# A later weight load, a fused x+1 and traced plan durations in an attention + MoE kernel

## The chip, the cores and the metric

The kernel runs on one core of one Trainium2 chip. The time is the device time of one execution in microseconds (us); most of what follows concerns differences of 1 to 13 us in about 1000. A profile is one execution with every instruction recorded; TensorE is PE there, its weight loads are PEld, VectorE is DVE, ScalarE is ACT, GpSimd is POOL, and SP is the engine that issues most DMAs.

## The reference, cut

```python
def phi(x): return np.where(x > 0, x, np.exp(x) - 1.0) + 1.0
q_p, k_p = phi(q), phi(k)                      # 8 batches, 8 heads, 576 tokens, 64 wide
kv = einsum('bhsd,bhde->...'); z = k_p.sum(2)  # linear attention
attn = num / (den + 1e-6)
x = attn as (4608, 512)
P = exp(x @ w_gate - max); 8 x: P /= P.sum(1); P /= P.sum(0); P *= N / E   # Sinkhorn
for e in range(8):                             # MoE, every expert on every token
    out += P[:, e:e+1] * (relu(x @ w1[e]) @ w2[e])
```

phi(x) is max(x + 1, min(exp(x), 1)), which is how the kernel computes it.

## The kernel before

A small planner in the kernel (`_Plan.run`) takes tasks with an engine, a planned duration, dependencies and a priority, plays them through in planned time and emits the instructions of each engine in that order. In the traces each engine works through its own stream in that order and waits for real data (a step shown below has TensorE stand 0.58 us at a column sum, with ready matmuls behind it). So a planned duration never delays anything by itself; it decides **where an instruction stands in its engine's stream**. If the plan believes that something is ready too early, the real engine stands still at that place, with ready work behind it.

The 16 attention steps `att(b, g)` (8 batches, two halves of the heads) have priority; expert 0's two layers fill TensorE in between; the Sinkhorn chain follows; then experts 1 to 7 run to the end. The parts that the change touches:

```python
for nm, ten in (("k", k), ("q", q), ("v", v)):        # the loads of step n; n = 2, 3 (batch 1) on POOL
    ti = fadd(("pool", 1.0) if n in (2, 3) else ("sp", 0.45), fn, acq=[gr], prio=pr,
              deps=[w_last[0] if n in (2, 3) else None, in_prev[0]])
# ... phi: exponential on ACT; x+1 on ACT or DVE; then min and max on DVE
def f_t(e, ...):                                       # x + 1
    if e == "dve": nc.vector.tensor_scalar(out=o, in0=gin[nm]["tile"], scalar1=1.0, ..., op0=ALU.add)
    else:          nc.scalar.add(out=o, in_=gin[nm]["tile"], add=1.0)
def f_m(_, ...):
    nc.vector.tensor_scalar(out=ge["tile"], in0=ge["tile"], scalar1=1.0, ..., op0=ALU.min)
    nc.vector.tensor_tensor(out=o, in0=o, in1=ge["tile"], op=ALU.max)
tt_ = fadd({"dve": 0.75, "act": 1.17}, f_t, ...)
tph[nm] = fadd(("dve", 1.15), f_m, deps=[te, tt_], ...)
# ... Sinkhorn, 8 times: f_a on DVE, f_c the column-sum matmul on TensorE, f_d on DVE
a = add(("dve", 2.1), f_a, ...); c = add(("pe", 0.2), f_c, ..., lat=0.2); last = [add(("dve", 0.5), f_d, ...)]
# ... the weights of expert 0: both matrices right behind batch 0
w_t = {0: load_w1(0, prio=-290.0, parts=2, deps=[vcast[0]]) + load_w2(0, prio=-280.0, parts=2, deps=[vcast[1]])}
```

The softmax here doesn't subtract the row's maximum and nothing guards it: scores larger than these inputs give would overflow.

## Time and profile before

| | before |
|---|---|
| time, median of 4 runs | 1007.62 us |
| span of the profiled run | 1005.3 us |
| TensorE busy | 970.7 us (97%) |
| TensorE idle, 23.2 to 140 us (29.30 + 87.50 less 23.51 + 83.94) | 9.35 us |
| first matmul of expert 1 starts at | 205.6 us |

TensorE is the bound. A caution about "busy": matmuls are pipelined. Four 512-column matmuls of one group take 0.863 us of TensorE's time when others follow, but the timeline shows such a group as some 1.03 us long, its end being modelled.

### The profile page before, as it was taken

The page shows a single profiled execution, that of the slowest core. Times are in us where ns is not written, and L with a number is a line of the kernel's source. Part 1 is how long each engine was busy: PE and PEld are TensorE (multiplying, and loading weights), DVE is VectorE, ACT ScalarE, POOL GpSimd, SP SyncE. Part 2 cuts the span into 40 slices and gives each one's busy share as a digit, 9 for nine tenths or more (in the row PEclk, how much of TensorE's full clock was granted, in tenths as well). Part 3 has the DMA queues.
Part 4 walks back from the last instruction along what each step waited for, and adds up shares of the span by engine and source line. Part 5 has one row for each costly group of instructions (what it writes and reads, how often), then busy time and mean ns, then how long its engine had stood idle before and what let it go on. Part 6 is the DMA issues. An engine that isn't in the chain of part 4 may idle for free.

```text
span 1005.3 us, 21388 instructions
## 1 busy us (share of the span) xinstructions
PE 970.7 (97%) x8716; PEld 791.7 (79%) x8716; DVE 773.5 (77%) x1555; ACT 566.9 (56%) x1040; POOL 132.5 (13%) x171
## 2 busy tenths in 40 slices
PE   7799998999999999999999999999999999999997
PEld 3456564478888888888888888888888888888885
DVE  6889869768777977788777977788777977777774
ACT  4888853565555555564555555555555555555552
POOL 4211100011111111111111111111111111111110
PEclk9999999999999999999999999999999999999999
DMA  9977953162223622272223522272223522226663
GB/s 262 331 260 248 265 150 127 62 121 75 74 74 89 143 74 75 74 158 74 74 75 95 138 74 74 75 158 74 75 75 101 131 75 74 75 89 163 160 162 100
DMA packets 47027, 121.98 MB, mean 121 GB/s; under 512 B 4176, under 2 KB 18000, under 8 KB 46928
## 3 DMA queue, kind: packets, MB, share of 16 engines
q1 hardware_dynamic: 32128, 99.76, 30.1%
q0 software_dynamic: 14480, 20.33, 11.4%
q8 instruction: 68, 1.11, 0.4%
q10 hardware_dynamic: 320, 0.52, 0.1%
q14 instruction: 31, 0.25, 0.1%
HBM read 119.69 MB, written 17.69 MB: 137 GB/s over the span
## 4 chain that ended last, share of the span: by engine, by line
PE 83%; DVE 13%; ACT 2%; issue 1%; DMA 0%; DVEq 0%; ACTq 0%
PE ye L797 31%; PE hq L618 22%; PE att L618 10%; PE Zye L618 5%; PE Zye L797 5%; PE ye L694 4%; PE hq L527 3%; ACT Zye L630 1%; DVE xn L369 1%; DVE xst L559 1%; DVE S L770 1%; DVE tq L275 1%; DVE tk L275 1%; DVE h L647 1%; PE xt_ps L380 1%
## 5 line engine op out<-in xcount | busy, mean ns | idle before, releaser
L811 DVE SCALAR_TENSOR_TENSOR acc<-ye,P_sb,acc 128x256 f32<-128x256 f32 x620 | 266.8, 478 | 90.7 <-PE ye L797 76.1
L618 PEld LDWEIGHTS <-W 128*128 128x128 f16 x2016 | 197.0, 98 | 34.3 <-issue 11.2
L797 PEld LDWEIGHTS <-S 128*128 128x128 f16 x1984 | 192.3, 98 | 27.4 <-DVE S L770 4.0
L797 PE MATMUL ye<-T,S 128*128 128x256 f16 x1488 | 192.6, 273 | 0.0
L821 POOL TENSOR_TENSOR acc<-acc,st 128x256 f32<-128x256 f32 x124 | 90.9, 753 | 639.2 <-ACT st L818 628.8
L618 PEld LDWEIGHTS <-w 128*128 128x128 f16 x1512 | 147.7, 98 | 21.4 <-issue 1.6
L797 PEld LDWEIGHTS <-h 128*128 128x128 f16 x1488 | 145.5, 98 | 17.2 <-issue 0.3
L618 PE MATMUL hq<-xs,W 128*128 128x256 f16 x1008 | 151.2, 273 | 6.5 <-ACT Zye L630 6.4
L618 PE MATMUL att<-xs,W 128*128 128x256 f16 x1008 | 151.2, 273 | 0.0
L618 PE MATMUL hq<-xs,w 128*128 128x256 f16 x1008 | 144.9, 272 | 1.0 <-DVE h L647 0.9
L644 ACT ACTIVATE h<-hq 128x512 f16<-128x512 f32 x126 | 76.3, 606 | 79.6 <-PE hq L618 79.6
L647 DVE CUSTOM_DVE_ANT_0 h<-att,s 128x512 f16<-128x512 f32 x126 | 86.6, 687 | 43.4 <-PE att L618 36.7
L770 DVE TENSOR_TENSOR S<-h 128x1024 f16<-128x1024 f16 x124 | 85.1, 686 | 40.9 <-ACT h L644 40.8
L641 ACT ACTIVATE h<-Zye 128x512 f16<-128x512 f32 x126 | 75.8, 602 | 53.8 <-PE Zye L618 53.8
L630 ACT COPY Zye<-hq 128x512 f32<-128x512 f32 x126 | 72.7, 577 | 57.7 <-PE hq L618 57.4
L638 ACT COPY s<-att 128x512 f32<-128x512 f32 x126 | 74.4, 590 | 46.3 <-PE att L618 46.1
L818 ACT ACTIVATE st<-Zye,P_sb 128x256 f32<-128x256 f32 x124 | 52.0, 470 | 75.1 <-PE Zye L797 75.1
L634 ACT COPY s<-hq 128x512 f32<-128x512 f32 x126 | 74.7, 593 | 25.1 <-PE hq L618 25.1
L647 DVE CUSTOM_DVE_ANT_0 h<-hq,s 128x512 f16<-128x512 f32 x126 | 86.2, 684 | 0.9 <-PE hq L618 0.3
L694 PE MATMUL ye<-w,h 128*128 128x512 f16 x320 | 76.8, 379 | 0.7 <-DVE acc L219 0.7
L618 PE MATMUL Zye<-xs,w 128*128 128x256 f16 x504 | 75.6, 273 | 0.0
L527 PE MATMUL hq<-xT,w 128*128 128x512 f16 x288 | 70.6, 379 | 0.3 <-ACT h L531 0.3
(90 smaller groups left out, 972.4 us busy)
## 6 DMA issues: line engine op xcount, KB each, us to landing
xs<-xd SPq DMA_DIRECT2D x63, 896.0 KB, 4.6
w<-in_moe_w_dram POOLq DMA_DIRECT2D x14, 1024.0 KB, 10.8
out_dram<-acc SPq DMA_DIRECT2D x68, 128.0 KB, 2.4
kin<-in_k_dram SPq DMA_DIRECT2D x14, 576.0 KB, 5.5
qin<-in_q_dram SPq DMA_DIRECT2D x14, 576.0 KB, 5.0
vin<-in_v_dram SPq DMA_DIRECT2D x14, 576.0 KB, 6.2
xd<-xst SPq DMA_DIRECT2D x9, 512.0 KB, 2.6
xd<-xT SPq DMA_DIRECT2D x9, 256.0 KB, 5.1
```

The costliest lines, as they stand in the source:

```text
L527: nc.tensor.matmul(ghq["tile"], lhsT=gw1["tile"][:, c, ts(f, P)], rhs=xT[:, c, ds(512 * g, 512)], start=(c == 0), stop=(c == NDT - 1))
L618: nc.tensor.matmul(dst[:, p, :], lhsT=lhs(p, c), rhs=rhs(c), start=(first and p == 0 and c == 0), stop=(c == 1), skip_group_check=True)
L630: nc.scalar.copy(out=Zt[1], in_=gX["tile"])
L634: nc.scalar.copy(out=gs2["tile"], in_=gX["tile"])
L641: nc.scalar.activation(out=hd(0, 0), in_=Zt[1], func=AF.Relu)
L644: nc.scalar.activation(out=hd(1, 0), in_=gX["tile"], func=AF.Relu)
L647: nc.vector._custom_dve(TENSOR_ADD_SAT, out=dst, in0=ps, in1=sb, s0=3.0e38, s1=0.0)
L694: nc.tensor.matmul(gy[tt]["tile"], lhsT=gh["tile"][:, f, ds(P * tt, P)], rhs=gw2["tile"][:, f, :], start=(f == 0), stop=(f == NFT - 1))
L770: nc.vector.tensor_tensor(out=Sx[:, i], in0=a0, in1=a1, op=op)
L797: nc.tensor.matmul(bank(g_)[:, s, :], lhsT=lhs(s, kk), rhs=rhs(kk), start=(new and s == 0 and kk == 0), stop=(kk == 3), skip_group_check=True)
L811: nc.vector.scalar_tensor_tensor(out=dst(), in0=bank(g_)[:, s, :], scalar=P_sb[:, gg, e:e + 1], in1=dst(), op0=ALU.mult, op1=ALU.add)
L821: nc.gpsimd.tensor_tensor(out=dst(), in0=dst(), in1=gst["tile"], op=ALU.add)
```

## The change

Its intent: bring batch 1's data in before the second weight matrix, which the filler needs later; take the x+1 off DVE's list as an instruction of its own; and give the planner durations that the trace shows.

```diff
-                      deps=[w_last[0] if n in (2, 3) else None, in_prev[0]])
+                      deps=[w_last[0] if n in (2, 3, 4) else None, in_prev[0]])
 ...
-    w_t = {0: load_w1(0, prio=-290.0, parts=2, deps=[vcast[0]]) + load_w2(0, prio=-280.0, parts=2, deps=[vcast[1]])}
+    w_t = {0: load_w1(0, prio=-290.0, parts=2, deps=[vcast[0]])}
+        if b == 1:
+            w_t[0] += load_w2(0, prio=-96.5, parts=2, deps=[in_prev[0]])
 ...
-                nc.vector.tensor_tensor(out=o, in0=o, in1=ge["tile"], op=ALU.max)
+                if g_["on"] == "act":
+                    nc.vector.tensor_tensor(out=o, in0=o, in1=ge["tile"], op=ALU.max)
+                else:
+                    for r in range(2):
+                        nc.vector.scalar_tensor_tensor(out=o[:, r], in0=gin[nm]["tile"][:, r], scalar=1.0,
+                                                       in1=ge["tile"][:, r], op0=ALU.add, op1=ALU.max)
-            tt_ = fadd({"dve": 0.75, "act": 1.17}, f_t, ...
-            tph[nm] = fadd(("dve", 1.15), f_m, ...
+            tt_ = fadd({"dve": 0.6, "act": 1.17}, f_t, ...        # on DVE it emits nothing any more
+            tph[nm] = fadd(("dve", 1.35), f_m, ...
 ... Sinkhorn
-            a = add(("dve", 2.1) ...  lat=0.2 ...  ("dve", 0.5)
+            a = add(("dve", 2.85) ... lat=0.15 ... ("dve", 0.65)
 ... smaller durations: state copies 0.22/0.24 -> 0.23/0.22, query copies 0.2+0.057j/0.12+0.113j -> 0.17+0.057j/0.12+0.1j,
     xn 0.1+0.28i -> 0.14+0.275i, logits' exponential 0.3 -> 0.24, x blocks 0.36 -> 0.42,
     expert 0's copy on ACT 0.65 -> 0.59, its scaling 0.35 -> 0.49
```

More of the change, by code (lines that the diff above doesn't have):

```diff
@@ L265, in f_t, with f_m @@
                 g_["tile"] = fp.tile([P, NJ, 2, D], FP16, tag="t" + nm, name="t" + nm)
-                o = g_["tile"].rearrange("p j r d -> p r j d")
-                if e == "dve":
-                    nc.vector.tensor_scalar(out=o, in0=gin[nm]["tile"], scalar1=1.0, scalar2=None, op0=ALU.add)
-                else:
-                    nc.scalar.add(out=o, in_=gin[nm]["tile"], add=1.0)
-            def f_m(_, ge=ge, g_=gt[nm]):
+                g_["on"] = e
+                if e == "act":
+                    nc.scalar.add(out=g_["tile"].rearrange("p j r d -> p r j d"), in_=gin[nm]["tile"], add=1.0)
+            def f_m(_, ge=ge, g_=gt[nm], nm=nm):
                 nc.vector.tensor_scalar(out=ge["tile"], in0=ge["tile"], scalar1=1.0, scalar2=None, op0=ALU.min)
                 o = g_["tile"].rearrange("p j r d -> p r j d")
-                nc.vector.tensor_tensor(out=o, in0=o, in1=ge["tile"], op=ALU.max)
+                if g_["on"] == "act":
[4 more added lines that the diff above has]
+                                                       in1=ge["tile"][:, r], op0=ALU.add, op1=ALU.max)
             te = fadd(("act", 1.17), f_e, deps=[tin[nm]], acq=[ge], use=[gin[nm]], prio=pr)
-            tt_ = fadd({"dve": 0.75, "act": 1.17}, f_t, deps=[tin[nm]],
+            tt_ = fadd({"dve": 0.6, "act": 1.17}, f_t, deps=[tin[nm]],
                        acq=[gt[nm]], use=[gin[nm]], prio=pr)
-            tph[nm] = fadd(("dve", 1.15), f_m, deps=[te, tt_], use=[ge, gt[nm]], prio=pr)
+            tph[nm] = fadd(("dve", 1.35), f_m, deps=[te, tt_], use=[ge, gt[nm], gin[nm]], prio=pr)
         gvv = S_.grp(p_vv)
@@ L311, in f_z @@
                     copy(e, gz["tile"][s, hh, rr, :], gkv[hh]["tile"][s, rr, :])
-                tz.append(fadd({"dve": 0.22, "act": 0.24}, f_z, deps=[tza, tkv], use=[gkv[hh], gz], prio=pr))
+                tz.append(fadd({"dve": 0.23, "act": 0.22}, f_z, deps=[tza, tkv], use=[gkv[hh], gz], prio=pr))
         gq = S_.grp(p_qpT)
@@ L330, in att @@
             t1 = fadd(("pe", 0.06 * (j1 - j0)), f_qt, deps=[tph["q"], tqa], acq=[gp], use=[gt["q"]], prio=pr)
-            tq.append(fadd({"act": 0.12 + 0.113 * (j1 - j0), "dve": 0.2 + 0.057 * (j1 - j0)}, f_qc, deps=[t1, tqa],
+            tq.append(fadd({"act": 0.12 + 0.1 * (j1 - j0), "dve": 0.17 + 0.057 * (j1 - j0)}, f_qc, deps=[t1, tqa],
                            use=[gp, gq], prio=pr))
@@ L372, in att @@
             t1 = fadd(("pe", 0.12 * (i1 - i0)), f_num, deps=[tden, txa], acq=[gn], use=[gq, gz], prio=pr)
-            txn.append(fadd(("dve", 0.1 + 0.28 * (i1 - i0)), f_xn, deps=[t1, trd, txa], use=[gn, grd, gxn], prio=pr))
+            txn.append(fadd(("dve", 0.14 + 0.275 * (i1 - i0)), f_xn, deps=[t1, trd, txa], use=[gn, grd, gxn], prio=pr))
         for c2 in range(2):
@@ L405, in logits @@
         x_users.append(t1)
-        lg_done.append(add(("act", 0.3), f_x, deps=[t1], use=[gl], prio=-50.0))
+        lg_done.append(add(("act", 0.24), f_x, deps=[t1], use=[gl], prio=-50.0))
     def sinkhorn():
@@ L446, in f_d @@
                 nc.vector.reciprocal(cc, Dc)
-            a = add(("dve", 2.1), f_a, deps=last, prio=-200.0)
-            c = add(("pe", 0.2), f_c, deps=[a], acq=[gc], prio=-200.0, lat=0.2)
-            last = [add(("dve", 0.5), f_d, deps=[c], use=[gc], prio=-200.0)]
+            a = add(("dve", 2.85), f_a, deps=last, prio=-200.0)
+            c = add(("pe", 0.2), f_c, deps=[a], acq=[gc], prio=-200.0, lat=0.15)
+            last = [add(("dve", 0.65), f_d, deps=[c], use=[gc], prio=-200.0)]
         def f_p(_):
@@ L559, in f_T @@
                 nc.vector.tensor_tensor(out=T[:, i], in0=a0, in1=a1, op=ALU.subtract)
-            last = add(("dve", 0.36), f_T, deps=deps + [t_close, last], acq=[gt_] if i == 0 else [], use=[gt_],
+            last = add(("dve", 0.42), f_T, deps=deps + [t_close, last], acq=[gt_] if i == 0 else [], use=[gt_],
                        prio=g - 8.0)
@@ L713, in unit_plain @@
             if e == 0:
-                tf = add({"act": 0.65, "dve": 0.69}, f_fin, deps=[ty[tt], t_close if g >= NA else None],
+                tf = add({"act": 0.59, "dve": 0.69}, f_fin, deps=[ty[tt], t_close if g >= NA else None],
                          use=[gy[tt]], prio=g - 400.0)
-                tf = add(("dve", 0.35), f_s, deps=[tf, p_done], prio=NG + g - 400.0)
+                tf = add(("dve", 0.49), f_s, deps=[tf, p_done], prio=NG + g - 400.0)
                 for dh in range(2):
```

## The prediction

The forecast's sum is 4.0 + 0.5 + 3.2 + 0.3 = 8.0 us, from 1007.6 to 999.6. Three things in the text need a word:

- "Zero saved on DVE" set an x+1 and a max, 0.67 us each, against a count for the fused pair. The profile before allows an estimate of the pair: the 36-element scalar_tensor_tensor takes 195 ns there and the 288-element fp32 tensor_tensor 457, a line through both gives 757 ns for 576 elements, and less the 0.08 us by which neighbours overlap (the x+1 at 7.36 takes 0.75 us, 0.67 to the next start) two make 1.35 us.
- "About 2 us lost at half clock" is an estimate: 4.32 us busy at 0.50 from 46.7 to 53.3 us. The same 18 kv matmuls take 1.10 us to the next group's start at 50.10, and 0.62 at 43.56, where the clock is 1.00.
- In the sum of 32 us for the second matrix, the 200 GB/s of the weights is as measured, whatever its reason; the last 2 us are my allowance, for which no figure of the profile is given.

> **What bounds the kernel now.** I read the page first, then the busy time of the engines in stretches that I cut where the work changes, then what TensorE waited for in each, then the timeline of the first 60 us. The page's first line settles the kind of kernel it is:
>
> ```profile
> PE 970.7 (97%) x8716; PEld 791.7 (79%) x8716; DVE 773.5 (77%) x1555; ACT 566.9 (56%) x1040; POOL 132.5 (13%) x171
> ```
>
> TensorE is occupied for 970.7 of 1005.3 us, so only 34.6 us of idle time exist to be won, plus whatever of the busy time is not real work. The stretches say where they lie (columns: stretch in us, its length, busy us of PE, PEld, DVE, ACT, POOL with instruction counts, granted clock, DMA share, GB/s):
>
> ```profile
> 0.00:23.20 23.20, 15.91 (x149) 8.61 (x150) 15.64 (x32) 9.35 (x16) 12.24 (x19) 1.00 1.01 249
> 23.20:52.50 29.30, 23.51 (x222) 13.78 (x220) 23.53 (x45) 23.45 (x35) 5.96 (x5) 0.90 0.97 331
> 52.50:140.00 87.50, 83.94 (x913) 52.33 (x913) 71.56 (x156) 73.08 (x120) 13.16 (x11) 0.99 0.76 230
> 140.00:180.00 40.00, 35.65 (x265) 17.52 (x264) 37.38 (x109) 16.19 (x30) 0.00 (x0) 1.00 0.43 163
> 180.00:1000.00 820.00, 811.44 (x7176) 699.50 (x7174) 624.41 (x1215) 444.85 (x843) 101.15 (x136) 1.00 0.35 97
> ```
>
> From 180 us on TensorE is 99% busy and the change touches nothing there. Before that the gaps are 7.3 us up to 23.2 (more in truth, since much of the busy time there is the 34 warm-up matmuls), 5.8 us from 23.2 to 52.5, 3.6 us to 140 and 4.35 us in the Sinkhorn stretch. Since the MoE matmuls after them run without a break to the end, each of these gaps that closes should come off the total one for one.
>
> Why is TensorE idle between 23.2 and 52.5? It has two kinds of work: attention, and expert 0's two layers as filler. At 23.2 only batch 0's tokens exist, enough for one group of 512 tokens: 8 x 4 matmuls of layer 1 and as many of layer 2, 0.863 us per four, 13.8 us in all. The last of these starts at 41.8 us. The second group needs batch 1's attention, whose transposed output is finished only at about 52.5. In between TensorE waits on the attention chain, and its clock halves:
>
> ```profile
> 44.00:46.00 2.00, 0.60 (x15) 0.32 (x10) 1.93 (x3) 1.18 (x3) 0.81 (x1) 1.00 0.90 248
> 46.00:48.00 2.00, 1.13 (x20) 1.06 (x21) 1.93 (x7) 1.51 (x3) 0.00 (x0) 0.65 0.88 326
> 48.00:50.00 2.00, 0.76 (x8) 0.50 (x5) 1.97 (x4) 1.73 (x2) 0.46 (x1) 0.50 0.72 236
> 50.00:52.00 2.00, 2.00 (x28) 1.70 (x27) 1.80 (x4) 1.45 (x3) 0.69 (x1) 0.50 0.79 260
> ```
>
> And batch 1 is late because its data is. In the timeline (start, length, engine, line, work) the second weight matrix is issued ahead of batch 1's first k, which DVE gets only at 26.25:
>
> ```profile
> 14.12 1.81 POOL L203 DMA_DIRECT2D w<-in_moe_w_dram  x2
> 15.91 0.72 POOL L249 DMA_DIRECT2D kin<-in_k_dram  x1
> ...
> 26.25 0.76 DVE L268 TENSOR_SCALAR tk<-kin 128x1152 f16<-128x1152 f32 x1 [2.40 <-DMA kin<-in_k_dram]
> 27.69 1.03 PE L694 MATMUL ye<-w,h 128*128 128x512 f16 x4
> ```
>
> The last row of that fence is the first matmul that needs the second weight matrix: it has landed by 27.7. In the Sinkhorn stretch, one wait is the whole story: the column-sum matmul sits in TensorE's ordered stream before DVE has its input.
>
> ```profile
> PE cs_ps L436 <- DVE gs L431: 4.2, 6, 1.0
> ```
>
> [...]
>
> **The change, part by part.**
>
> *Load order.* Removed from before batch 1: the second matrix's time on the DMA engines. The DMA view of the first 60 us gives what landed in 40 slices of 1.5 us:
>
> ```profile
> GB/s 0 123 390 393 410 396 393 279 204 202 208 186 195 139 186 372 421 399 387 384 387 317 392 387 389 246 312 318 265 283 252 350 191 346 217 323 292 286 232 335
> ```
>
> Inputs run at about 390 GB/s; the weights, from 10.5 to 22 us, at about 200 GB/s of landed fp16[...]. So the second matrix's 1.05 MB takes about 5.2 us. Batch 1's issue moves up by about 4.7 us (it no longer waits for the second v cast and two weight issues), and its k should be usable near 20.5 instead of 26.25. The price: 3.54 MB of batch 1 (six loads of 576 KB, about 9 us at 390 GB/s) now precede the weights. Without competition the second matrix lands at about 10.5 + 5.2 + 9 + 5.2 + 2 = 32 us; batch 2's k, q, v, whose buffers come free near 22 to 25 and whose SP queue does not really wait for the weights (only the planner believes that), add about 4.5 us. So its first half lands at 31 to 35 and the second at 34 to 38. TensorE reaches layer 2 after layer 1 (6.9 us) and the first half of batch 1's attention (2.5 us: 9 transposes, 18 kv, 10 den, 10 num and 10 output matmuls at the pace of the timeline, 0.5 + 0.6 + 0.3 + 0.6 + 0.5), at 31 to 33. I expect a stall of 0 to 4 us there, against 5.8 us of gaps plus about 2 us lost at half clock (some 4 us busy at 0.50 from 46.7 to 53.3) that go away. Net 4.0 us gained, with batch 1's output ready near 45.
>
> *Fused phi.* The DVE path loses an x+1 (about 0.67 us start to start) and a max (0.67)[...]. That is zero saved on DVE. The add also moves from beside the exponential to behind it, 0.67 us longer on a critical phi, but DVE has fewer places to be delayed: the 1.71 us x+1 at 13.08 in the start chain disappears. At the start I count 0.5 us gained, later nothing, because from 52.5 to 140 TensorE is the bound and not DVE.
>
> *Traced durations.* The planner thinks a Sinkhorn step takes 2.1 + 0.2 + 0.2 + 0.5 us plus 0.3 of latencies, 3.3 us; the trace shows a period of 4.4 (148.19 to 152.69). Its column-sum matmul is thus placed about 1 us early in TensorE's order, the 0.6 to 1.0 us waits seen six times. With 2.85 and 0.65 the planned step is 4.1 us. I expect 3.2 of the 4.2 us back. The other new durations differ by under 0.15 us; they reshuffle the 3.6 us of small gaps up to 140, which I put at +0.3 us gained.
>
> Sum: 4.0 + 0.5 + 3.2 + 0.3 = 8.0 us, so 1007.6 - 8.0 = 999.6.
>
> **Rivals.** (1) *The weight wait takes over.* If layer 2 stands in TensorE's order before the second matrix is there, the ordered stream also holds up batch 1's attention behind it.[...] Against: TensorE has about 9 us of other work first. A 6 us stall[...] leaves the first part at zero or minus 2: 1004 to 1006. (2) *DVE and ACT become the bound.* Both are 8 to 9 tenths busy from 30 to 120 us, and the fused op makes each phi's last step longer.[...] Against: the DVE sums are equal, and attention's 14 us per batch (seven batches from 26 to 127) is below TensorE's some 20 us per batch (attention's 5 plus 1.125 groups of 13.8; a batch has 576 tokens). This costs 1 to 2 us at most: 1001. (3) *The weight load hides completely* and the half-clock stretch disappears: 7.8 us from the front, 4 from Sinkhorn, 1 from the start give 995. (4) *Reordering luck*: a new list order may create new in-order stalls worth 1 to 3 us either way.
>
> **Range and chances.** Total gain above is capped by roughly 5.8 + 2 + 4.2 + 1.5 = 13.5 us, 994; the poor outcome is Sinkhorn's 3 us alone, 1004.5. I take 994.5 to 1005. A gain over 2% needs 20 us, which would need nearly every gap up to 180 us to close, start included: 0.02. A loss over 2% needs 20 us of new gaps: 0.01. Within 2%: 0.97.
>
> **What will show it.** Right: first k of batch 1 used on DVE near 20 to 21 us; granted clock 1.00 in the stretch 44 to 54; the second layer-1 group starting near 45; cs_ps waits on gs under 1.5 us in total; unchanged idle after 180. Wrong: TensorE idle over 5 us between 30 and 40 with layer 2 as what waits; DVE's sum up to 140 us rising by more than 3 us; batch 1's output not earlier than 50; new waits on DVE in 52.5 to 140 above 5 us in total.

## The result, and the profile after

The changed kernel takes 994.46 us (median of 4 runs, 993.22 to 997.64), the kernel before 1007.62 in the same rounds. The ratio is 0.9873, with a 95% interval of 0.9849 to 0.9897. A ratio here is the mean time of one kernel's runs over that of the other's in the same rounds, so it is not quite the ratio of the medians quoted. Later it gave 994.33 against 1008.22, ratio 0.9862. So the gain is 13 to 14 us, where 8 were predicted.

The page's line of busy time for the changed kernel, then its stretches, cut as before (stretch, length, busy us of PE, PEld, DVE, ACT, POOL, granted clock, DMA share, GB/s):

```profile
PE 965.9 (97%) x8716; PEld 789.4 (80%) x8716; DVE 771.6 (78%) x1561; ACT 562.5 (57%) x1034; POOL 131.6 (13%) x171
```

```profile
0.00:23.20 23.20, 17.09 (x151) 8.85 (x152) 15.44 (x34) 10.42 (x15) 11.66 (x19) 1.00 0.97 302
23.20:52.50 29.30, 26.26 (x292) 15.50 (x291) 24.59 (x52) 24.80 (x42) 5.99 (x5) 1.00 0.97 293
52.50:140.00 87.50, 84.33 (x966) 52.91 (x965) 73.19 (x165) 69.25 (x114) 12.60 (x11) 1.00 0.80 242
140.00:180.00 40.00, 40.00 (x198) 19.42 (x197) 36.80 (x105) 19.78 (x34) 0.00 (x0) 1.00 0.39 152
180.00:1000.00 820.00, 798.22 (x7115) 692.71 (x7113) 621.58 (x1208) 438.21 (x832) 101.32 (x136) 1.00 0.35 96
```

The number of instructions is the same on TensorE (8716). What went is idle time: from 23.2 to 52.5 us it is 3.0 us instead of 5.8, in the Sinkhorn stretch zero instead of 4.35. The first matmul of expert 1 starts at 192.5 instead of 205.6 us, 13.1 us earlier, and the whole span is 13.9 us shorter (991.4 against 1005.3): nearly everything was gained before expert 1.

Listed idle time up to 180 us fell by 8.7 us, less than that, so I counted work instead. By 180 us expert 0's 512-column matmuls number 495 in the profile after and 434 before; 61 more at 0.863 / 4 us is 13.2 us of work. By 140 us the lead is 18 of them, 3.9 us, and the changed kernel has also finished all the logits, of which the old one still has three groups to do. With two warm-up matmuls among them, which the changed kernel has behind it too, they take 3.1 us of TensorE in the old timeline (139.96 to the start of the next matmul at 143.09). So **the front gained 7.0 us and the Sinkhorn stretch 6.1.**

The POOL timeline after shows the new load order. The profile puts the wait of its last row, the gate weights' issue, down to the landing of batch 1's first k, which dates that landing to about 20.05 us:

```profile
11.10 0.72 POOL L249 DMA_DIRECT2D kin<-in_k_dram  x1
...
16.56 0.72 POOL L249 DMA_DIRECT2D vin<-in_v_dram  x1
17.27 0.77 POOL L203 DMA_DIRECT2D w<-in_moe_w_dram  x1
18.51 0.75 POOL L203 DMA_DIRECT2D w<-in_moe_w_dram  x1 [0.48 <-DMA w<-in_moe_w_dram]
20.05 0.74 POOL L467 DMA_DIRECT2D wg_sb<-in_moe_w_gate_dram  x1 [0.79 <-DMA kin<-in_k_dram]
```

Yet the exponential of that k starts only at 23.31, since on ACT it stands behind two copies of batch 0's output:

```profile
22.24 1.18 ACT L217 COPY xT<-xt_ps 128x576 f16<-128x576 f16 x2 [3.05 <-PE xt_ps L383]
23.31 1.18 ACT L262 ACTIVATE ek<-kin 128x1152 f16<-128x1152 f32 x1
```

The stretch that had a clock of 0.65 and 0.50 before (same columns as above) now has 1.00, and TensorE is busy for 1.53 to 2.00 of each 2 us, where it was 0.60 to 1.13 from 44 to 50:

```profile
44.00:46.00 2.00, 1.80 (x30) 1.20 (x28) 1.86 (x6) 1.76 (x6) 0.00 (x0) 1.00 0.99 378
46.00:48.00 2.00, 2.00 (x46) 1.52 (x44) 2.00 (x4) 2.00 (x5) 0.00 (x0) 1.00 1.03 394
48.00:50.00 2.00, 2.00 (x38) 1.39 (x37) 1.93 (x5) 1.98 (x7) 0.58 (x1) 1.00 0.81 240
50.00:52.00 2.00, 1.53 (x12) 0.86 (x11) 1.94 (x6) 1.98 (x3) 0.65 (x1) 1.00 0.81 237
```

The first matmul of layer 2, the one that needs the late matrix, waits for nothing (TensorE's timeline after), and the view of waits lists none for these weights later either:

```profile
34.43 1.02 PE L699 MATMUL ye<-w,h 128*128 128x512 f16 x4
```

**Why the Sinkhorn stretch gave 6 us where the view of waits lists 4.2.** One step of it in TensorE's timeline, first before, then after (start, length, work; idle time and its releaser in brackets):

```profile
153.83 1.03 PE L694 MATMUL ye<-w,h 128*128 128x512 f16 x4
155.44 0.39 PE L436 MATMUL cs_ps<-gs,ones_t 128*128 128x8 f32 x2 [0.58 <-DVE gs L431]
155.68 1.02 PE L527 MATMUL hq<-xT,w 128*128 128x512 f16 x4
```

```profile
156.41 1.03 PE L532 MATMUL hq<-xT,w 128*128 128x512 f16 x4
157.28 0.28 PE L439 MATMUL cs_ps<-gs,ones_t 128*128 128x8 f32 x2
157.42 2.75 PE L532 MATMUL hq<-xT,w 128*128 128x512 f16 x12
```

Before, the group at 153.83 uses 0.863 us of TensorE, to 154.69, and the next 512-column matmul starts at 155.68: the column sum cost 0.99 us. After, the same subtraction, 157.42 less 157.27, gives 0.15. The step lost 0.84 us and the view of waits listed 0.58 of it. The 0.26 us in between are the modelled tail of the last matmul, shown as busy, and the start-up of the column sum's two matmuls, which with nothing in front of them take 0.24 instead of 0.14 us until the next may start. A step can lose time this way without any wait being listed: for the column sum at 159.44 before, none is, and it cost 0.55 us (159.14 to 159.69, counted the same way).

### The profile page after: what moved, and what is told of

Same layout as the page of the kernel before. It is cut to its first block, busy times and chain, and to the rows that moved or that the text cites. A ratio compares the mean times of both kernels' runs of the same rounds, so it can differ in the third digit from the quotient of the medians.

```text
span 991.4 us, 21411 instructions
## 1 busy us (share of the span) xinstructions
PE 965.9 (97%) x8716; PEld 789.4 (80%) x8716; DVE 771.6 (78%) x1561; ACT 562.5 (57%) x1034; POOL 131.6 (13%) x171
## 4 chain that ended last, share of the span: by engine, by line
PE 88%; DVE 6%; ACT 3%; DMA 1%; issue 1%; SPq 0%; ACTq 0%; DVEq 0%
PE ye L802 32%; PE hq L623 22%; PE att L623 10%; PE ye L699 6%; PE Zye L623 5%; PE Zye L802 5%; PE hq L532 4%; ACT Zye L635 1%; DVE tk L277 1%; DMA kin<-in_k_dram 1%; DVE tq L277 1%; DVE S L775 1%; DVE xn L372 1%; PE xt_ps L383 1%; DVE h L652 1%
```

## The experiments

The diff falls into four independent parts: the load order, the fused phi (with its two durations), the three Sinkhorn durations, and the smaller durations. I put each alone on the kernel before, and took each alone off the changed kernel, 5 rounds each. "Idle" is TensorE's from 23.2 to 140 us, "expert 1" the start of its first matmul, both of the profiled run.

| run | median us | before | ratio | 95% interval | idle us | expert 1 at us |
|---|---|---|---|---|---|---|
| load order alone | 1003.06 | 1007.51 | 0.9956 | 0.9940 to 0.9971 | 6.6 | 200.1 |
| Sinkhorn durations alone | 1001.29 | 1007.51 | 0.9941 | 0.9927 to 0.9954 | 9.0 | 199.5 |
| fused phi alone | 1010.50 | 1007.51 | 1.0025 | 1.0011 to 1.0038 | 9.5 | 206.2 |
| smaller durations alone | 1005.72 | 1007.51 | 0.9981 | 0.9969 to 0.9993 | 9.3 | 204.2 |
| all but the fused phi | 999.01 | 1008.57 | 0.9911 | 0.9897 to 0.9926 | 8.4 | 196.6 |
| all but the load order | 1002.38 | 1008.57 | 0.9938 | 0.9925 to 0.9952 | 10.2 | 200.3 |
| all but Sinkhorn | 998.86 | 1008.57 | 0.9910 | 0.9893 to 0.9926 | 6.4 | 198.1 |
| all but the smaller durations | 1001.13 | 1008.22 | 0.9934 | 0.9921 to 0.9947 | 9.6 | 197.9 |
| the whole change, again | 994.33 | 1008.22 | 0.9862 | 0.9849 to 0.9874 | 6.7 | 193.6 |

### Each part alone

**Load order alone:** the first two and the `if b == 1` hunks of the diff.

> The kernel before with the load order alone. My theory: the front stretch (23.2 to 52.5 us) loses its half-clock part and most of its 5.8 us of TensorE gaps, worth 5 to 7 us: 1000.5 to 1002.5 us, batch 1's first k in use before 25 us, granted clock 1.00 from 44 to 54 us, and the 4.2 us of column-sum waits still there. Rival, that the reshuffled plan and not the data's arrival made the gain: within 2 us of before, 1005.5 to 1008.

Measured: 4.45 us by the medians, a little under the range I gave. DVE reads batch 1's first k at 23.22 instead of 26.25 us, the clock is 1.00 from 23.2 to 52.5, batch 1's attention output is done at 46.0 instead of 52.5 us and the idle time falls by 2.8 us. The rival of an unrelated reshuffle falls. The weight wait that I named as a danger does appear here, as the view of TensorE's waits shows (total, times, longest), beside 3.2 us of the column-sum waits:

```profile
PE cs_ps L436 <- DVE gs L431: 3.2, 6, 0.9
PE qt_ps L325 <- DVE tq L275: 2.8, 1, 2.8
PE ye L696 <- DMA w<-in_moe_w_dram: 1.4, 1, 1.4
```

**Sinkhorn durations alone:**

```diff
-            a = add(("dve", 2.1), f_a, deps=last, prio=-200.0)          # and 0.2 -> 0.15, 0.5 -> 0.65
+            a = add(("dve", 2.85), f_a, deps=last, prio=-200.0)
```

> The kernel before with the three Sinkhorn durations alone. My theory: the column-sum waits go from 4.2 us to under 0.5, and because each wait also exposes the tail of a pipelined matmul, the time falls by about 6 us, to 1001 to 1002.5. Rival, that only the listed waits come back: 3.5 to 4.3 us, 1003.3 to 1004.1. The front to 140 us is as before in both.

Measured: 6.2 us by the medians; the profile lists no column-sum wait, and up to 140 us the plan is that of before (296 of the 512-column matmuls done in both; by 180 us 463 against 434, 29 x 0.216 = 6.3 us). The rival that only the listed 4.2 us come back falls. This is the cleanest result.

**Fused phi alone:** the hunks of `f_t`, `f_m` and their two durations.

> The kernel before with the fused phi alone (and its two planned durations). My theory: no gain on DVE[...]: 1006 to 1009 us, DVE busy up to 140 us within 2 us of before. Rival, that freeing DVE of the x+1 speeds up the attention of batch 1: 1001 to 1004 and TensorE's gaps from 23.2 to 52.5 us under 4 us.

Measured: 3.0 us slower, 1.5 us beyond my own upper end and far from the rival. DVE's busy time up to 140 us is 109.6 us against 110.7. (The profiles show 0.76 us for an x+1, for a max and for one fused op.) Batch 1's output comes no earlier (52.9 us), and the clock is at half over a longer stretch: 0.56 from 44 to 46 us and 0.50 to 54, where before it was 0.65 from 46 to 48 and 0.50 to 52. Within this kernel's six runs the time follows the mean granted clock: 1007.56 us at 0.996, 1011.53 at 0.988. The profiled one is among the quickest (1008.10). Which of the two, the clock or the waiting, brings the other along is not shown.

**Smaller durations alone:** only the numbers at the end of the diff.

> The kernel before with the other traced durations alone (no Sinkhorn, no fuse, no order). My theory: a reshuffle worth 1 us either way, 1006.5 to 1008.5. Rival, that these durations carry part of the gain: 1005 or less.

Measured: 1.8 us faster, between the two expectations. Alone, the four parts give a product of ratios of 0.9956 x 0.9941 x 1.0025 x 0.9981 = 0.9903, some 9.7 us; the change made 13. With intervals of about 1.3 us on each part, that difference alone is hardly clear of noise. That the parts interact shows in the runs below, which take one part off.

### Each part taken off the change

**All but the fused phi:** `f_t`, `f_m` and their durations as before, in the changed kernel.

> The changed kernel with phi unfused again (and its two planned durations as before). The fuse alone cost 3.0 us. Theory A, that the parts do not interact: this beats the changed kernel by about 3 us, 990 to 993. Theory B, that the fuse pays only once the data is early (the four parts alone sum to 9.5 us and the change made 13.1): 996 to 999, TensorE's gaps from 23.2 to 52.5 us above 3 us and a wait for the weights as in the load order alone.

Measured: 999.01 us. That is Theory B's time, but its mechanism is not the one at work: no weight wait returns and the gaps from 23.2 to 52.5 stay small (2.9 us). The idle time grows after that, from 3.2 to 5.4 us between 52.5 and 140, and the first layer-1 matmul starts at 24.0 instead of 22.3 (22.9 in the change's second profile). So the same edit that costs 3 us on the old kernel is worth 4 to 5 in the new one. It is not only the instruction that changes: the plan also does 19 of the 32 x+1 on DVE with the fuse and 23 without, the others on ACT.

**All but the load order:** the three order hunks undone.

> The changed kernel with the old load order. Without interaction: 4.5 us slower than the changed kernel, 998 to 1000. If the order is what the other front parts need: 1001 to 1004, with the half-clock stretch near 44 to 54 us back in both cases.

Measured: 1002.38 us, ratio 0.9938, 6.6 to 7.7 us worse than the change by the ratios (0.9873 and 0.9862). The second reading holds. The half-clock stretch is back (0.50 from 48 to 52 us, 0.66 from there to 56) and batch 1's output is at 51.3.

**All but Sinkhorn:** the three durations undone.

> The changed kernel with the old Sinkhorn durations. The Sinkhorn stretch is apart from the front, so theory: 6 us slower than the changed kernel as in the run alone, 999.5 to 1002, column-sum waits of 3 to 4.5 us back. If the interaction lies here: under 3 or over 9 us slower.

Measured: 998.86 us, 3.7 to 4.8 us worse by the ratios, with 3.6 us of column-sum waits. That is less than the 6.2 alone. In the profiled runs the step is 4.5 us (193.6 to 198.1 at expert 1's first matmul). The three durations change nothing up to 140 us here either, and the intervals of the two runs overlap, so a real difference between 6.2 and this is not shown.

**All but the smaller durations:** those numbers undone.

> The changed kernel without the smaller traced durations (the copies, xn, logits, T, final scale). Alone they gave 1.8 us. Without interaction: 1 to 3 us slower than the changed kernel of this call. If these small numbers matter mainly by the order that they happen to give, anything from 3 us faster to 5 slower, with no column-sum waits either way.

Measured: 1001.13 us, 6.8 us worse than the change, outside what I had allowed for. The stretches of its profile (columns as before) show where: TensorE is busy for only 2.13 of 4.00 us from 44 to 48, and in the next 4 us the clock is 0.70.

```profile
44.00:48.00 4.00, 2.13 (x37) 1.58 (x34) 3.61 (x9) 3.14 (x6) 0.00 (x0) 1.00 0.89 308
48.00:52.00 4.00, 3.56 (x69) 2.35 (x70) 2.81 (x8) 3.90 (x8) 1.18 (x1) 0.70 0.76 257
```

Batch 1's output is ready at 46.65 us instead of 52.5 (44.1 in the change), but the data's early arrival is not enough. Durations that differ by 0.01 to 0.14 us give another order, with less work for TensorE from 44 to 50 us; which of them does it was not tested.

### Is it the fused instruction, or the order that its durations give?

The changed kernel, with the order of all engines untouched, but the x+1 and the max written apart in the place of the fused pair:

```diff
-                    for r in range(2):
-                        nc.vector.scalar_tensor_tensor(out=o[:, r], in0=gin[nm]["tile"][:, r], scalar=1.0, ...
+                    nc.vector.tensor_scalar(out=o, in0=gin[nm]["tile"], scalar1=1.0, scalar2=None, op0=ALU.add)
+                    nc.vector.tensor_tensor(out=o, in0=o, in1=ge["tile"], op=ALU.max)
```

> The changed kernel with its plan and the order of every engine untouched, but each fused pair written as the x+1 and the max of before, back to back in the same place. If the fused op as such is worth something, this is 2 us or more slower than the changed kernel of the same call. If only the new order that its planned durations give is, it is within 1.5 us. By my count both take 1.34 us of DVE start to start, so I expect the second.

Measured: 998.02 us (995.18 to 998.32) against 994.33 for the change; ratios 0.9892 and 0.9862. I expected the second outcome and got the first by the number: a difference of 3.0 us by the ratios, of which the spread of the four and four runs leaves about 1 to 5.

The trace does not show where these 3 us would come from. The profile caught the fast run of the four (995.18), and there expert 1 starts at 193.7 us, against 193.6 in the change's profile. Nor does DVE take longer for the split form. The x+1, which does not need the result of the min before it, starts 0.37 us after the min does (25.02 to 25.39); the fused op, which does need it, starts 0.52 us after (24.51 to 25.03). From the start of the min to the start of the next instruction DVE takes 1.84 us with the split pair (25.02 to 26.86) and 1.87 with the fused one (24.51 to 26.38). The three runs at 998 have a clock of 0.997 and no trace, and the change itself has a run at 994.34 with that clock. So that the instruction as such is worth 3 us is suggested by the times and explained by nothing here; it stays open.

### Does the halved clock cost anything?

The kernel before, with 72 dummy matmuls ahead of four groups that waited between 43 and 50 us, for example:

```diff
+            for _i in range(14 if n == 4 else 0):
+                nc.tensor.matmul(gkv[0]["tile"]..., lhsT=warm[:, 0:P], rhs=warm[:, 0:2 * D + 2], start=True, stop=True)
             for j in range(NJ):
```

> The kernel before, with 72 dummy matmuls of 128 to 130 columns put in front of four groups that waited 0.8 to 1.4 us each between 43 and 50 us, no other order changed. If the half clock comes from TensorE's low activity there, the clock stays at 1.00 longer and the time falls by 1 to 3 us, 1004.5 to 1006.5. If the gaps alone count and the halved clock costs nothing, within 0.5 us of before or slower.

Measured: 1008.15 us against 1008.22, ratio 1.0002 (0.9989 to 1.0014), although the clock is full where it had been 0.65 and 0.50, as its stretches show:

```profile
46.00:48.00 2.00, 1.88 (x40) 1.81 (x38) 1.91 (x5) 1.55 (x3) 0.00 (x0) 1.00 0.73 264
48.00:50.00 2.00, 1.40 (x22) 1.28 (x22) 1.93 (x6) 1.73 (x3) 0.00 (x0) 1.00 0.30 79
```

So from 46 to 50 us the clock was 0.65 and 0.50 with TensorE busy for 1.13 and 0.76 of 2 us, and 1.00 with the dummies and 1.88 and 1.40; by what rule it falls is not shown. Nor does the run say what the half clock costs, because the dummies cost time themselves. They write into the tile of the group behind them, so they wait for that tile to be released, as the group did (47.55 and 49.80 us before, with the same releasers). In TensorE's timeline of this run two of the four sets, 34 matmuls, run only after the wait, in front of the real work (L368 the dummies, L371 the real ones):

```profile
48.21 0.94 PE L368 MATMUL num_ps<-warm 128*128 128x128 f16 x14 [0.34 <-DVE qpT L219]
48.99 0.62 PE L371 MATMUL num_ps<-kvz,qpT 128*128 128x128 f16 x8
50.34 1.28 PE L368 MATMUL num_ps<-warm 128*128 128x128 f16 x20 [0.73 <-DVE xn L376]
51.46 0.28 PE L371 MATMUL num_ps<-kvz,qpT 128*128 128x128 f16 x2
```

They put 0.78 and 1.12 us, 1.9 in all, into the attention chain, and DVE stands for 0.89 us behind the last set. Yet from the end of the q's max on DVE to the end of batch 1's output that chain took 6.56 us (46.46 to 53.02), where it took 6.53 before (45.92 to 52.45). If nothing else differs, the full clock gave back about what the dummies cost. From these 1.9 us I estimate the half clock at up to 2 us here; the run itself shows only that both together come to zero, within 1.4 us.

### An attempt at a better version

The changed kernel, with the x+1 apart again for the first step only, where DVE has nothing to do during the first exponential:

```diff
+                elif n < NU:      # NU = 1
+                    nc.vector.tensor_scalar(out=..., in0=gin[nm]["tile"], scalar1=1.0, scalar2=None, op0=ALU.add)
```

> The changed kernel, with x+1 apart again for the first of the 16 steps only, where DVE stood idle for 4.26 us before the first exponential ended. Theory: the start chain is 0.5 to 1 us shorter, 993 to 994.5, first layer-1 matmul up to 1 us before 22.3. Rival: the fused pairs beside the v casts (2.25 and 2.37 us instead of 1.43) are the delay, and the first step is not: within 0.5 us of the changed kernel.

Measured: 995.69 us, ratio 0.9876, the same as the change within the interval. The start chain is indeed 1.3 us shorter, more than expected. TensorE's timeline shows how the gain is given back:

```profile
21.05 0.99 PE L537 MATMUL hq<-xT,w 128*128 128x512 f16 x3
...
24.80 1.02 PE L537 MATMUL hq<-xT,w 128*128 128x512 f16 x4 [1.36 <-ACT h L541]
26.17 0.69 PE L307 MATMUL kv_ps<-vv,tk 64*128 64x130 f16 x18 [0.35 <-DVE tk L282]
28.00 0.68 PE L333 MATMUL qt_ps<-ident,tq 128*128 128x128 f16 x9 [1.14 <-DVE tq L282]
```

These rows start at 22.32, 26.07, 27.03 and 28.34 in the changed kernel: a lead of 1.27, 1.27, 0.86 and 0.34 us. TensorE goes on standing behind the relu, which ACT does after two exponentials of batch 1, and then waits for batch 1's phi. No run beats the change clearly.

## Why the prediction was right or wrong

**The bound.** Right. TensorE's lost time before expert 1 was what could be won, and what was won there came off the total: 13.1 us at expert 1's first matmul, 13.9 in the span. (That the change touches nothing after 180 us is not quite so: expert 0's scaling and the x blocks lie there too.) Idle after 180 us is as before (waits of 8.0 us listed, 8.2 before).

**The range.** The median, 994.46, lies at its very lower edge (994.5), 0.04 us beyond it. The mechanism and the direction of the three gains from the load order, the Sinkhorn durations and the smaller ones were right; the sum of 8.0 was too small by 5, and three terms of it were mis-sized.

**"I expect 3.2 of the 4.2 us back"** (Sinkhorn). Mis-sized: 6.2 us alone, 6.1 by the count of matmuls inside the change. I took the listed waits for the whole loss. Each step also loses a modelled tail and the start-up of the column sum, 0.26 us in the step shown above; eight times that and the 4.2 us make 6.3. (The period that I read as 4.4 us, from 148.19 to 152.69, is 4.50.)

**"Net 4.0 us gained"** (load order). Right alone (4.45), and its stall of 0 to 4 us is the 1.4 us of that run. Inside the change the wait is absent: the third layer-2 group, which with the order alone stands waiting until 38.58 us, starts at 38.57 with other work in front of it. Batch 1's output was ready at 44.1, where I wrote 45. The term "about 2 us lost at half clock" stays open, since the run with the dummies did not isolate it. That run does show the clock at 1.00 where it had been 0.65 and 0.50, with TensorE kept busier; the longest wait listed from 43 to 50 us in the profile before is 1.40 us. One reading was wrong: I took the v cast at 38.73 for batch 1's last, held back by the SP loads of batch 2. It is batch 2's first. Batch 1's last starts at 33.91 and waits 3.41 us for TensorE to free its buffer, not for a DMA. So the old trace does not show that the SP loads held batch 1 back.

**"At the start I count 0.5 us gained, later nothing"** (fused phi). Wrong in a way that no single number repairs: 3.0 us lost on the old kernel, 4 to 5 us won in the new. That nothing is saved on DVE was right: the pair takes 1.34 us start to start (6.71 to 8.05 us in the profile after), as much as the x+1 and the max, and 1.43 from start to end; one fused op takes 757 ns (median, 576 elements). Two pairs took longer, 2.25 us at 8.54 and 2.37 at 12.22, both beside POOL's casts of v (8.06 to 9.51 and 12.54 to 13.99); in the profile before, a max at 8.52 took 1.58 us and an x+1 at 13.08 took 1.71 instead of 0.76, beside those casts too. What makes them longer is not shown. The count of DVE time says nothing about the plan: taking the x+1 out as an instruction of its own also moves what stands behind it and which x+1 go to ACT. How much of the 4 to 5 us is that and how much the instruction stays open (the split pair in the same place lost 3 us by the times and nothing in the trace). The start did shorten, by 0.7 us alone (22.5 for 23.2) and by 0.9 us in the change (22.3; 22.9 in its second profile), so 0.5 was near.

**"+0.3 us"** (smaller durations). Mis-sized: 1.8 us alone and 6.8 as the last piece. I judged a duration by how far it was off, under 0.15 us. By these runs what counts seems to be whether it flips an order that TensorE then has to wait for.

**Interaction.** I added the parts. Taking any front part off the change costs 3.8 to 7.7 us by the ratios, while alone they give -3 to +4.5, 3.3 together, where the front of the change gained 7.0. The table's idle column tells the same: 6.6 us with the order alone, 6.2 to 6.7 in the change, but 8.4, 9.6 and 10.2 with one front part missing. TensorE is fed between 24 and 60 us only when data, DVE order and filler order fit together. That the interaction lies in which order the planner happens to find is argued from these runs, not shown piece by piece.

**The marks.** Clock 1.00 from 44 to 54, column-sum waits under 1.5 us (none), DVE's sum up to 140 us (113.2 against 110.7, under the 3 us that I had set): as predicted. "First k of batch 1 used on DVE near 20 to 21 us" failed: by that wait the data landed at 20.05, but ACT's stream had it wait to 23.31, and the op on DVE that reads this k starts at 25.03. The second layer-1 group started at 47.28 where I had said 45.

**The rivals.** The weight wait is real and small (1.4 us, in one run). DVE or ACT as the new bound: not seen, apart from waits of 2.2 us in all for a relu on ACT (the longest 1.4). Rival (3), the best case of 995, is the one that came true: the weight load hides completely, the half-clock stretch is gone, and the size fits. Its shares were off, 8.8 us for front and start against 7.0, and 4 for Sinkhorn against 6.1, so that the sum fits is partly luck. "Reordering luck" (4) was put at 1 to 3 us; the smaller durations reach 6.8.

## What to carry to other kernels

Where a plan fixes the order of each engine, take its durations from a trace, even the small ones: they cost nothing, and values that were 0.75 and 0.15 us too small in a chain of eight steps cost 6 us here. Count lost TensorE time by the start of the next useful matmul and not by the listed waits: in the step shown above they give 0.58 us of 0.84. Don't add up the worth of parts that share a scheduler. And where dummy work is to test what a slow clock costs, look in the trace whether it really runs inside the waits: here half of it ran after them.
